# Two attentions in one static schedule: B's loads one transpose at a time, B's query features later to their banks, and new priorities

## The chip, the cores and the metric

The kernel runs on one core of one Trainium2 chip. The metric is the device time of one execution in microseconds (us). The profile is one execution recorded by the hardware profiler. Engine names are those of the profile: PE (matrix engine, PEld its weight loads), DVE (vector), ACT (scalar), POOL (GpSimd) and SP (the queue that issues nearly all DMAs).

## What is computed

Two independent attention layers, A and B, each with 2048 tokens, width 512, 32 heads of 16. Their outputs stand side by side in the result.

```python
# A: full softmax attention
qkv = (x @ wqkv) -> q, k, v per head
p = softmax(q k^T / 4)               # 32 heads x 2048 x 2048
out_A = (p v) @ wo
# B: linear attention with learned features
phi_q = [softmax(q w_phi), softmax(-q w_phi)]     # 32 features per head
phi_k = the same of k
kv, z = sum over s of phi_k v, phi_k
out_B = (phi_q kv / (phi_q z + 1e-6)) @ wo
```

## The kernel before, in words

**A's tiling.** The work of A is cut into 32 units, a unit being 4 heads and 512 queries, `units[u] = (g, c)`. Each unit has 16 key tiles of 128 keys. For one key tile, PE forms the scores of the four heads (L642), the scores are exponentiated, and PE multiplies them with V (L657) into one PSUM bank per unit. Eleven or more of the 16 tiles of a unit go through ACT: `act_kt` makes two halves, each of two score matmuls into one of two bank pairs (`A_bank`, PSUM banks 0 to 3) and one exponential of 128x1024 on ACT (L757). The other tiles go through DVE: `dve_kt` makes four score matmuls into single banks (the pool `G`, banks 4 to 7), four conversions (L795) and three adds (L806) that together approximate the exponential. In the whole program 758 exponentials are on ACT, and 133 tiles (532 conversions, 399 adds) are on DVE.

**The end of a unit.** `make_unit_end` copies the unit's bank to `X` (L704, DVE). Then a chain over the SP queue follows: `sums<-X` (L710, DMA), reciprocal `rin<-sums` (L713, DVE), `scr<-rin` (L716, DMA), four broadcasts `Yd<-scr` (L719, DMA), a multiply on POOL (L726), for odd units four more DMAs `OT<-Oo` (L733), and after 8 units the output projection (L849), its copy (L853) and its store (L857). The reciprocal stands in DVE's own queue, which runs in order, so DVE can do nothing else while that DMA has not landed.

**B's work.** It is laid into A's as filling. `start_b` issues B's loads on SP: the small `BDr` (L901), 8 transposing loads of the query and key weights (L902), 4 transposing loads of B's input, 512 KB each (L905), and two plain loads (L907, L909). They go into buffers that A's projections have just finished with (`w`, `xT`), so they start when A's last projection is done. After them come 8 folds of the feature map into the weights (`fold`, L917 and L921), 16 key steps (`k_step`: L933 features, L936 exponentials, L946 scaling on POOL, L955 values, L966 the sum over keys), and then the query part: `qf_step` (L995 features on PE, L999 exponentials on ACT) and 16 `q_step`s (L1009 on PE, L1019 and L1022 on DVE, L1036 to L1046 on POOL, the transpose L1052 on PE, its copy L1055 on ACT, the output projection L1058 on PE, its copy L1062 on DVE and its store L1065). B's steps are released in proportion to how many of A's 512 key tiles have been placed; the fractions are `B_AT`.

**What sets the order.** `_Sched` places tasks at build time. Each engine has several streams (queues) of tasks with a weight each; for every engine the scheduler takes, among the first tasks of its streams, the one with the smallest start plus weight, with assumed durations and latencies. The order that results is fixed into every engine's instruction queue; on the chip only semaphores are waited for. A task of PE that would delay the next A score pair beyond its due time gets 0.4 added (L238 to L242). Where PE would be idle, matmuls on zeros keep it busy (L684).

**B's load tasks before.** One load task holds all its DMAs, so nothing of A's can stand between them on SP:

```python
return put(sp_b, _Task("sp", us * n, dma(d, lambda e, t, i: fn(e, i), n), deps, lat=lat))   # us=0.5
```

**The query features before.** The PE task of `qf_step` depends on B's input and the folded weights alone and takes a bank of `G`; the two exponentials that free this bank depend in addition on `bs["kend"]`, the end of the key part.

Of the kernel before, what the change touches and what calls it, by code (L numbers as in the profile page):

```python
# [151 lines left out]
class _Sched:  # L152
# [10 lines left out]
    FORCE = 0.40  # L163

    def __init__(self):
        self.free = {}
        self.busy = {}
        self.streams = {}
        self.end = 0.0
        self.mode = None  # L170
        self.rows = [0.0] * 4
        self.port = {"dve": 0.0, "pool": 0.0}
        self.urgent = None
        self.last_port = None
        self.filler = None
        self.active = collections.deque()
        self.nfill = 0
        self.nforce = 0
# [38 lines left out]
    def _choose(self, eng, ss):  # L217
        cand = []
        for s in ss:
            if not s["q"] and s["src"] is not None:  # L220
                s["src"](s)
            if s["q"]:
                t = s["q"][0]
                if t.prep is not None:
                    t.prep(t)
                r = self._ready(t) if t.gate is None or t.gate() else None
                if r is not None:
                    if s is not self.urgent:
                        r += self.SLACK.get(eng, 0.0)
                    st = self._start(t, r)  # L230
                    w = s["w"]
                    cand.append([st, st + (w(t) if callable(w) else w), s, r])
        if not cand:
            return None
        if eng == "pe" and self.urgent is not None:
            u = [c for c in cand if c[2] is self.urgent]
            if u:
                due = max(u[0][3], self.free["act"] - self.MM - self.PE_LAT)  # L238
                for c in cand:
                    t = c[2]["q"][0]  # L240
                    if t.mode != "r" and c[0] + t.dur + self.SWITCH > due + 0.02:
                        c[1] += 0.4  # L242
        c = min(cand, key=lambda c: c[1])
        return c[0], c[2]
# [91 lines left out]

_LOG2E = 1.4426950408889634
# [6 lines left out]
def _main_path(nc, es, P, dsem, flag, A_x, A_wqkv, A_wo, B_x, B_wqkv, B_w_phi, B_wo, out):  # L344
# [6 lines left out]
    B_AT = (0.24, 0.54, 0.95)  # L351
# [80 lines left out]
    pe_qa = SC.stream("pe", -0.02)  # L432
    SC.urgent = pe_qa
    pe_tp = SC.stream("pe", -0.15)
    pe_qd = SC.stream("pe", lambda t: -0.05 if SC.mode == "r" else 0.25)
    pe_pj = SC.stream("pe", -0.03)
    pe_pa = SC.stream("pe", left_in(pt_sl, 2, 0.1))
    pe_pd = SC.stream("pe", left_in(rj_sl, 1, 0.1))
    pe_b = SC.stream("pe", 0.02)
    pe_op = SC.stream("pe", -0.03)  # L440
    one_bank = [pe_tp, pe_pj, pe_b, pe_op, pe_pa, pe_pd]
    ac_ev = SC.stream("act", -0.1)
    ac_xe = SC.stream("act", -0.2)
    ac_ex = SC.stream("act", 0.0)
    dv_x = SC.stream("dve", -0.4)
    dv_xe = SC.stream("dve", -0.3)
    dv_ev = SC.stream("dve", -0.2)
    dv_op = SC.stream("dve", -0.2)
    dv_n = SC.stream("dve", -0.15)
    dv_a = SC.stream("dve", -0.1)  # L450
    dv_ad = SC.stream("dve", 0.0)
# [3 lines left out]
    dv_ek = SC.stream("dve", -0.1)  # L455
# [28 lines left out]
    def put(s, t):  # L484
        s["q"].append(t)
        return t
# [128 lines left out]
    at = []  # L615
    for g in range(1, 4):
        for c in range(4):
            at.append((32 * (g - 1) + 8 + 4 * c, lambda g=g, c=c: proj("k", g, c)))
        at.append((32 * (g - 1) + 10, lambda g=g: proj("q", g, 0)))
    for i in range(12):  # L620
        at.append((22 + 5 * i, lambda i=i: proj("q", i % 4, 1 + i // 4)))
# [12 lines left out]
    state = {"ua": 0, "ud": 0, "n": 0}  # L634
# [112 lines left out]

    def act_kt(u, kt):
        exps = []
        for half in range(2):  # L750
            qk = qk_task(u, kt, half, [("A", A_bank, 1, 1)], lambda t, i: 2 * t.res["A"].idx + i)
            qk_all[u].append(qk)
            put(pe_qa, qk)

            def ex_emit(e, t, qk=qk):
                b = 2 * qk.res["A"].idx
                return e.activation(pT[:, t.res["p"].idx, :], PS[:, b:b + 2, :].rearrange("p a n -> p (a n)"),  # L757
                                    ACT.Exp, scale=0.25)
            exps.append(put(ac_ex, _Task("act", 0.92, one("act", ex_emit), [qk], lat=AL,
                                         need=[("p", pt_sl, 1, 1)], rel=[lambda qk=qk: [qk.res["A"]]])))  # L760
        put(pe_pa, pv_task(u, exps + [v_ready[kt]],
                           lambda h: VP[:, kt, v0(h):v0(h) + 32],
                           lambda r: pT[:, exps[r // 2].res["p"].idx, 512 * (r % 2):512 * (r % 2) + 512],
                           [lambda: [exps[0].res["p"], exps[1].res["p"]]]))
        close(u)
# [59 lines left out]
    def src_d(_):  # L825
        u = max(state["ud"], state["ua"])
        while u < NU and (not d_rem[u] or (u == state["ua"] and len(a_rem[u]) + len(d_rem[u]) < 4)):
            u += 1
        if u >= NU or u > state["ua"] + 1:
            return  # L830
        if u > state["ua"] and len(a_rem[u - 1]) + len(d_rem[u - 1]) > 3:
            return
        state["ud"] = u
        g, c = units[u]
        for n, kt in enumerate(d_rem[u]):
            if k_ready[(g, kt // 4)].done and q_ready[(g // 2, c)].done and vj_ready[(kt, 3)].done:
                dve_kt(u, d_rem[u].pop(n))
                return
# [47 lines left out]
    pe_kf, pe_v, pe_kv, pe_qf, pe_y, pe_t, pe_o = (SC.stream("pe", x) for x in (-0.03,) * 7)  # L886
    dv_f, dv_red, dv_v, dv_kv, dv_y, dv_d, dv_ob = (SC.stream("dve", x) for x in (-0.2, -0.1, -0.12, -0.12, -0.12, -0.12, -0.15))
    dv_mn = SC.stream("dve", 0.05)
    ac_kf, ac_qf, ac_ot = (SC.stream("act", x) for x in (-0.1,) * 3)
# [5 lines left out]
    def b_load(name, fn, n, deps, lat, us=0.5):  # L895
        d = dsem(name)
        return put(sp_b, _Task("sp", us * n, dma(d, lambda e, t, i: fn(e, i), n), deps, lat=lat))

    def start_b():
# [4 lines left out]
            B_wqkv[:, (i // 4) * 512 + (i % 4) * 128:(i // 4) * 512 + (i % 4 + 1) * 128]), 8, freed, 18.0)  # L904
        b_x = b_load("xb", lambda e, i: e.dma_start_transpose(  # L905
            xT[:, i, :], B_x[0][:, i * 128:(i + 1) * 128]), 4, freed, 25.0)
# [5 lines left out]
            mask8[:].unsqueeze(1).unsqueeze(3).broadcast_to([128, 4, 8, 16]), ALU.mult)), [b_bd], pre=[t_m8], lat=GL))  # L912
# [3 lines left out]
        def fold(x, ct):  # L916
            f = put(pe_b, _Task("pe", 0.24, pe_group(4, lambda e, t, i: e.matmul(  # L917
                PS[:, t.res["b"].idx, i * 128:(i + 1) * 128], w[:, i, x * 512 + ct * 128:x * 512 + (ct + 1) * 128],
                BD[:, i, :], start=True, stop=True)), [b_wt, bd], lat=PL, need=[("b", G, 1, 1)]))
# [11 lines left out]
        def k_step(st):  # L931
# [3 lines left out]
                [b_x] + wf[1], [("b", G, 1, 2), ("e", ek_sl, 1, 2)])  # L935
# [9 lines left out]
            for a in range(2):  # L945
# [11 lines left out]
                [b_x, b_wv, bs["vb1"]], [("b", G, 1, 1), ("v", vb_sl, 1, 1)])  # L957
# [35 lines left out]
        def qf_step(cq, t4):  # L993
# [3 lines left out]
                [b_x] + wf[0], [("b", G, 1, 2), ("e", et_sl, 1, 8)])  # L997
            for a in range(2):
                ets[(cq, 2 * t4 + a)] = f, put(ac_qf, _Task("act", 0.49, one("act", lambda e, t, a=a: e.activation(  # L999
                    eT_b[f.res["e"].idx][:, a, :], bank_of(f), ACT.Exp, scale=1.0 - 2.0 * a)),  # L1000
                    [f2] + bs["kend"], lat=AL, rel=[lambda: [f.res["b"]]]))

        def q_step(st):
# [41 lines left out]
            for k in range(2):  # L1045
# [14 lines left out]
                [te, b_wo], [("b", G, 1, 1)])  # L1060
# [1033 lines left out]
```

## Time and profile before

Three runs took 824.21, 830.3 and 833.1 us; the median is 830.3 us. The profiled execution has a span of 829.5 us and a mean granted PE clock of 0.959.

| engine | busy us | share of the span |
|---|---|---|
| PE | 759.9 | 92% |
| ACT | 751.4 | 91% |
| DVE | 736.3 | 89% |
| POOL | 157.3 | 19% |

The profile cuts the span into stretches, and gives for each the busy time of each engine, the granted PE clock (1.00 is full speed) and what the DMA engines moved. Idle time of ACT, which is the length of a stretch less ACT's busy time in it, sums as follows:

| stretch, us | what happens | ACT idle, us |
|---|---|---|
| 0 to 60 | loads, A's first projections | 16.4 |
| 60 to 160 | A, further projections | 2.0 |
| 160 to 195 | A, last projections, B's first loads | 5.8 |
| 195 to 210 | B's input is loaded | 11.1 |
| 210 to 240 | folds, first key step | 6.3 |
| 240 to 790 | A with B's key and query part | 3.6 |
| 790 to 829.5 | last unit of A, last query steps of B | 33.1 |

Mean durations of single instructions (pitch in a row where several follow each other): exponential of A on ACT 0.93 us (13 in 12.05 us), conversion on DVE 0.62 us (4 in 2.47 us), add on DVE 0.63 us (3 in 1.89 us), group of four value matmuls on PE 0.23 us. The issue of a transposing load holds SP for 1.26 us (weights, median of 8) or 2.36 us (input, median of 4).

### The profile page before, as it was taken

What the parts mean: (1) busy time and instruction counts of PE and PEld (TensorE: products, weight loads), DVE (VectorE), ACT (ScalarE), POOL (GpSimd) and SP (SyncE); (2) the same over time, 40 slices, a digit from 0 to 9 for tenths busy, and PEclk for the clock granted to TensorE, in tenths of its full rate; (3) what the DMA queues carried; (4) which work ended last, traced back from release to release, by engine and by line L of the source; (5) the groups of instructions that cost most, each with busy time, mean ns of one, the idle gap of its engine ahead of it and who ended that gap; (6) DMA issues with size and microseconds to landing.
All of it is one profiled execution on the core that took longest, in us unless ns stands there. A gap on an engine that the chain in (4) does not pass through costs nothing.

```text
span 829.5 us, 17394 instructions
## 1 busy us (share of the span) xinstructions
PE 759.9 (92%) x7165; PEld 231.7 (28%) x7249; DVE 736.3 (89%) x1306; ACT 751.4 (91%) x856; POOL 157.3 (19%) x233
## 2 busy tenths in 40 slices
PE   8999999994999998999989999999999999999963
PEld 3332222221222222222222222223332222332231
DVE  2699999884698999989999999999989999999973
ACT  6879999884699999999999999999999999999930
POOL 5211011110112012221121021005222102302051
PEclk9999999997599999999999999999999999999976
DMA  7100000027000000000000000000000010001001
GB/s 150 54 8 9 11 5 8 8 48 168 7 9 10 14 19 15 12 8 11 10 4 9 27 18 9 12 8 18 15 8 18 14 22 17 20 26 31 9 23 51
DMA packets 44154, 19.61 MB, mean 24 GB/s; under 512 B 33312, under 2 KB 42016, under 8 KB 44064
## 3 DMA queue, kind: packets, MB, share of 16 engines
q1 hardware_dynamic: 42480, 17.60, 8.8%
q8 instruction: 59, 0.97, 0.5%
q10 hardware_dynamic: 1584, 0.79, 0.4%
q14 instruction: 31, 0.25, 0.1%
HBM read 7.88 MB, written 4.46 MB: 15 GB/s over the span
## 4 chain that ended last, share of the span: by engine, by line
ACT 59%; PE 24%; DVE 11%; SPq 3%; issue 1%; DMA 1%; POOL 0%; ACTq 0%; POOLq 0%
ACT pT L757 55%; PE PS L642 8%; PE PS L657 7%; DVE rg L795 6%; DVE rg L806 3%; PE PS L570 3%; ACT e_k L936 2%; PE PS L567 1%; ACT eT L999 1%; SPq L905 1%; SPq L902 1%; PE PS L1058 1%; PE PS L684 1%; ACT e_k L1055 1%; PE PS L525 1%
## 5 line engine op out<-in xcount | busy, mean ns | idle before, releaser
L757 ACT ACTIVATE pT<-PS 128x1024 bf16<-128x1024 f32 x758 | 708.6, 1079 | 32.8 <-PE PS L642 28.2
L642 PE MATMUL PS<-QT,KT 32*128 32x512 bf16 x2048 | 352.0, 389 | 21.7 <-ACT pT L757 13.1
L795 DVE TENSOR_SCALAR rg<-PS 128x512 uint16<-128x512 f32 x532 | 340.5, 680 | 18.1 <-PE PS L642 16.1
L806 DVE TENSOR_SCALAR rg<-rg 128x2048 uint16<-128x2048 uint16 x399 | 260.6, 693 | 4.6 <-PE PS L657 4.1
L642 PEld LDWEIGHTS PS<-QT,KT 32*128 32x128 bf16 x2048 | 89.5, 91 | 302.4 <-ACT pT L757 218.0
L657 PE MATMUL PS<-rg,VJ 128*32 128x512 f16 x1596 | 147.9, 389 | 11.0 <-DVE rg L806 10.7
L657 PE MATMUL PS<-pT,VP 128*32 128x512 bf16 x1516 | 151.7, 397 | 2.2 <-ACT pT L757 1.1
L657 PEld LDWEIGHTS PS<-pT,VP 128*32 128x32 bf16 x1516 | 38.3, 94 | 87.4 <-issue 65.8
L726 POOL TENSOR_TENSOR OT<-X,Yd 128x256 bf16<-128x256 f32 x32 | 22.7, 727 | 198.4 <-DVE rg L806 155.3
L946 POOL TENSOR_TENSOR w<-e_k,stat 128x512 bf16<-128x512 bf16 x32 | 33.2, 1056 | 136.1 <-DVE rmin L952 42.6
L657 PEld LDWEIGHTS PS<-rg,VJ 128*32 128x32 bf16 x1596 | 39.0, 95 | 68.4 <-issue 31.5
L657 PE MATMUL PS<-rg,VP 128*32 128x512 f16 x532 | 53.2, 390 | 0.0
L726 POOL TENSOR_TENSOR Oo<-X,Yd 128x256 bf16<-128x256 f32 x32 | 23.1, 738 | 108.1 <-DMA Yd<-scr 55.2
L1036 POOL TENSOR_TENSOR w<-w 128x272 f32<-128x272 f32 x32 | 23.8, 760 | 98.5 <-DVE w L1022 80.3
L570 PE MATMUL PS<-xT,w 128*128 128x512 bf16 x111 | 30.6, 383 | 3.5 <-issue 1.9
L1055 ACT ACTIVATE e_k<-PS 128x512 bf16<-128x512 bf16 x16 | 10.1, 631 | 20.8 <-PE PS L1052 20.8
L684 PE MATMUL PS<-ones_t,zer 128*32 128x512 bf16 x276 | 28.4, 409 | 0.0
L704 DVE COPY X<-PS 128x512 f32<-128x512 f32 x32 | 22.0, 686 | 4.8 <-PE PS L657 3.6
L1022 DVE TENSOR_TENSOR w<-PS,stat 128x408 f32<-128x408 f32 (+1 forms) x48 | 25.2, 526 | 0.6
L1046 POOL TENSOR_TENSOR w<-w,den 128x256 bf16<-128x256 f32 x32 | 19.8, 636 | 31.3 <-DVE rg L806 9.3
L1058 PE MATMUL PS<-woB,e_k 128*128 128x512 bf16 x50 | 17.5, 435 | 4.6 <-issue 1.8
L939 DVE TENSOR_REDUCE stat<-e_k 128x64 f32<-128x1024 bf16 x16 | 19.3, 1209 | 0.1
(85 smaller groups left out, 422.8 us busy)
## 6 DMA issues: line engine op xcount, KB each, us to landing
Yd<-scr SPq DMA_DIRECT2D x128, 32.0 KB, 1.8
out_dram<-OA SPq DMA_DIRECT2D x16, 128.0 KB, 1.7
out_dram<-e_k SPq DMA_DIRECT2D x16, 128.0 KB, 1.7
OT<-Oo SPq DMA_DIRECT2D x64, 16.0 KB, 1.8
w<-in_A_wqkv_dram SPq DMA_DIRECT2D x2, 384.0 KB, 4.9
OT<-in_A_x_dram SPq DMA_DIRECT2D x1, 512.0 KB, 4.6
w<-in_A_wqkv_dram ACTq DMA_DIRECT2D x1, 512.0 KB, 7.7
WOp<-in_A_wo_dram SPq DMA_DIRECT2D x1, 512.0 KB, 6.8
```

The lines of the kernel that those rows point to most:

```text
L570: return e.matmul(bank_of(t), w[:, ct, c0:c0 + 128], xT[:, ct, c * 512:(c + 1) * 512], start=(ct == 0), stop=(ct == 3))
L642: return e.matmul(out_ap, KT[32 * r:32 * r + n, g, kt * 128:(kt + 1) * 128], QT[32 * r:32 * r + n, c, g // 2, :], start=True, stop=True, t ...
L657: return e.matmul(PS[32 * r:32 * r + 32, pvb[u].idx, :], lhs(8 * (g // 2) + 2 * r + g % 2), rhs(r), start=t.res["first"], stop=t.res["last ...
L684: P.op("pe", lambda e, r=r: e.matmul(PS[32 * r:32 * r + 32, pvb[u].idx, :], zer[:], ones_t[:].unsqueeze(1).broadcast_to([128, 4, 128]), st ...
L726: ms.append(put(po_n, _Task("pool", 0.65, one("pool", lambda e, t, cs=cs: e.tensor_tensor(OT[:, c % 2, g // 2, cs] if even else Oo[:, ms[0 ...
L757: return e.activation(pT[:, t.res["p"].idx, :], PS[:, b:b + 2, :].rearrange("p a n -> p (a n)"), ACT.Exp, scale=0.25)
L795: return e.tensor_scalar(rg[:, q0.res["i"].idx, 512 * r:512 * r + 512], PS[:, qk.res["D"].idx, :], ya, yb, ALU.mult, ALU.add)
L806: ad = put(dv_ad, _Task("dve", 0.59, one("dve", lambda e, t, j=j: e.tensor_scalar(rg[:, t.res["j"].idx, :], rg[:, q0.res["i"].idx, :], flo ...
L946: ph.append(put(po_phi, _Task("pool", 1.0, one("pool", lambda e, t, a=a: e.tensor_tensor(pk[ph[0].res["k"].idx][:, 512 * a:512 * a + 512]. ...
L1022: muls.append(put(dv_y, _Task("dve", 0.485, one("dve", lambda e, t, yv=yv, lo=lo, n=n: e.tensor_tensor(ysv[r0.res["y"].idx][:, 136 * lo:13 ...
L1036: ad = [put(po_y, _Task("pool", 0.65, one("pool", lambda e, t, k=k: e.tensor_tensor(y3(0)[:, 2 * k:2 * k + 2], y3(0)[:, 2 * k:2 * k + 2], ...
L1058: o1, o2 = two_step(pe_o, lambda e, t, i: e.matmul(bank_of(t), oT_b[tp.res["t"].idx][:, i, :], woB[:, i, :], start=(i == 0), stop=(i == 3) ...
```

## The change

The change has four parts.

**Loads.** `b_load` makes one task per DMA, with issue times of 1.32 us (weights) and 2.5 us (input) instead of 0.5, so that DMAs of A can stand between them in SP's order:

```diff
-        return put(sp_b, _Task("sp", us * n, dma(d, lambda e, t, i: fn(e, i), n), deps, lat=lat))
+        return [put(sp_b, _Task("sp", us, dma(d, lambda e, t, r, i=i: fn(e, i)), deps, lat=lat)) for i in range(n)]
...
-            B_wqkv[:, (i // 4) * 512 + (i % 4) * 128:(i // 4) * 512 + (i % 4 + 1) * 128]), 8, freed, 18.0)
+            B_wqkv[:, (i // 4) * 512 + (i % 4) * 128:(i // 4) * 512 + (i % 4 + 1) * 128]), 8, freed, 4.0, 1.32)
...
-            xT[:, i, :], B_x[0][:, i * 128:(i + 1) * 128]), 4, freed, 25.0)
+            xT[:, i, :], B_x[0][:, i * 128:(i + 1) * 128]), 4, freed, 8.0, 2.5)
```

**Query features.** The wait for the end of the key part moves from the exponentials to the PE task, so the bank is taken only then:

```diff
-                [b_x] + wf[0], [("b", G, 1, 2), ("e", et_sl, 1, 8)])
+                b_x + wf[0] + bs["kend"], [("b", G, 1, 2), ("e", et_sl, 1, 8)])
...
-                    [f2] + bs["kend"], lat=AL, rel=[lambda: [f.res["b"]]]))
+                    [f2], lat=AL, rel=[lambda: [f.res["b"]]]))
```

**Due time of A's score pairs.** The due time now counts the score pairs that are done but whose exponential is not placed yet, and the surcharge for being late is 0.346:

```diff
-                due = max(u[0][3], self.free["act"] - self.MM - self.PE_LAT)
+                due = max(u[0][3], self.free["act"] + self.EXP * self.ahead() - self.MM - self.PE_LAT - _W["early"])
...
-                        c[1] += 0.4
+                        c[1] += _W["guard"]
```

**Weights and constants.** All stream weights now come from one table `_W` (for instance PE's transposes -0.288 for -0.15, B's folds 0.111 for 0.02, B's output projection 0.067 for -0.03). `B_AT` becomes (0.24, 0.54, 0.917) for (0.24, 0.54, 0.95); A's late query projections are released every 5.753 tiles for 5 (`p2`); `lead` is 2 for 3. A function `third` would let A's score pair take two banks of `G`, if at least `spare` = 9 slots of `G` were free:

```diff
+        if pair + 0.3 < own and sum(x.left == 0 for x in G) >= _W["spare"]:
+            t.need = [("A", G, 2, 1)]
```

## The prediction

> **What bounds the kernel now.** I read the slices first. ACT, DVE and PE all stand at 9 nearly everywhere, so three engines are close to full; a hole at slices 9 to 12 and the end are the exceptions.
>
> ```profile
> PE   8999999994999998999989999999999999999963
> DVE  2699999884698999989999999999989999999973
> ACT  6879999884699999999999999999999999999930
> PEclk9999999997599999999999999999999999999976
> ```
>
> The chain that ended last is 59% ACT, and 55% of the span is one line, A's exponential. From 240 to 790 us ACT idles 3.6 us in all. So this kernel is ACT's 751.4 us of busy time plus ACT's idle time, 78 us, and the change is worth what it takes from or adds to these 78 us.
>
> ```profile
> L757 ACT ACTIVATE pT<-PS 128x1024 bf16<-128x1024 f32 x758 | 708.6, 1079 | 32.8 <-PE PS L642 28.2
> ```
>
> Of the 32.8 us idle before A's exponentials, 28.2 are waits for scores. The timeline shows the largest of them, and what stands behind it (start us, length us, engine, line; in brackets the idle time before it and its releaser):
>
> ```profile
> 190.64 9.43 SPq L905 DMA_TRANSPOSE xT<-in_B_x_dram  x4
> ...
> 190.81 0.68 DVE L704 COPY X<-PS 128x512 f32<-128x512 f32 x1
> ...
> 201.53 0.62 SPq L710 DMA_DIRECT2D sums<-X  x1
> 206.02 0.25 DVE L713 RECIPROCAL rin<-sums 128x16 f32<-128x16 f32 x1 [11.53 <-DMA sums<-X]
> ...
> 206.88 0.62 PE L657 MATMUL PS<-rg,VJ 128*32 128x512 f16 x4 [10.74 <-DVE rg L806]
> ...
> 208.07 2.96 ACT L757 ACTIVATE pT<-PS 128x1024 bf16<-128x1024 f32 x3 [11.08 <-PE PS L642]
> ```
>
> The copy X is done at 191.5, but its DMA waits on SP for four transposes and two plain loads and is issued at 201.5. The reciprocal waits 11.53 us at the head of DVE's queue; PE waits for DVE, ACT for PE. After it the stretches (busy PE, PEld, DVE, ACT, POOL, then the granted clock, DMA share, GB/s) show a second loss:
>
> ```profile
> 195.00:200.00 5.00, 1.14 (x15) 0.20 (x7) 0.00 (x0) 1.99 (x3) 0.00 (x0) 0.91 1.12 218
> 200.00:205.00 5.00, 0.00 (x0) 0.00 (x0) 0.00 (x0) 0.00 (x0) 0.00 (x0) 0.50 0.99 261
> ...
> 215.00:220.00 5.00, 5.00 (x35) 2.40 (x34) 2.81 (x5) 3.43 (x4) 0.00 (x0) 0.50 0.00 0
> 220.00:225.00 5.00, 5.00 (x35) 1.42 (x32) 3.85 (x6) 3.42 (x4) 1.00 (x1) 0.50 0.00 0
> ```
>
> Until about 229 us PE runs at half clock, is full (5.00 of 5.00), and ACT gets only 3.4 of 5. The hole costs ACT 11.1 us at 195 to 210 and 6.3 after it, 17.4 in all.
>
> **What the skill says.** "Perfetto Trace Analysis", section Tensor Engine Instruction, calls ACT, DVE and GpSimd strict first-in first-out; the 11.53 us at the reciprocal agree. "DMA: Bandwidth & Descriptors", Queues, rings and completion order, says each DMA engine consumes descriptors in ring order; this agrees with `sums<-X` landing 4.47 us after its issue at 201.5 (chain of waits), against at most 2.4 for the last unit (issued 793.25, used 795.69). The same page, Latency and other measured facts, gives 261 GB/s for a transposing DMA; the row at 200 to 205 moves 261. "TensorE: Matmul & The Clock Gate", What's actually happening, states half clock after an idle window of about 3.4 us and full clock after a busy one. The fall agrees (0.50 from 200 us on), the recovery doesn't: it took some 22 us of busy PE. I price with the trace.
>
> **The change part by part.** Work is not changed: both orders hold 758 exponentials, 532 conversions, 399 adds, the same DMAs; only the zero matmuls differ (292 for 276). Steady ACT work therefore stays at 751.4 us, and each part is priced in ACT idle.
>
> *Loads, with the new time of release.* In the new order of SP, unit 5's `sums<-X` stands behind three weight transposes, unit 6's behind the third input transpose, with the fourth after it. The wait this adds is SP's: what queues behind a transpose is the next A DMA, and DVE's reciprocal waits for that. Unit 5 in the worst case: 3 x 1.34 us issue (10.71 / 8), 0.6 own issue, 4.5 landing = 9.1, against 4.4 us of DVE work that the new order has between the copy and the reciprocal (7 instructions of about 0.62), so 4.7 stall. Unit 6: 2.4 + 0.6 + 4.5 = 7.5 against 4.6, so 2.9. Best case for both is 0, for the scheduler now knows 1.32 and 2.5 us per issue. I take 1.5 each, 3 in all (0 to 8). B's consumers have room: the first fold stands about 6.9 us of DVE work (6 conversions, 5 adds) and more after unit 5's reciprocal, while the last two weight transposes need 0.35 + 2.6 + 2.7 = 5.7 us from there; the first key step comes 24 exponentials (22 us) after the first fold. Without a long PE hole the half clock and its 6.3 us go too. Gain 17.4 - 3 = 14.4.
>
> *Start and projections (weights, `p2`).* ACT idles 24.2 us up to 195 us, at least 8 of it before anything can be exponentiated (first A exponential at 11.5 us). PE is 96% busy up to 160 us, so PE's order sets it. In the new order 84 projection matmuls instead of 100 stand ahead of the 32nd exponential's scores (16 x 0.216 = 3.5 us of PE), and up to the 160th there are 24 value matmuls (6 groups x 0.23 = 1.4), 9 DVE scores (about 0.1 each, 0.9) and 56 zero matmuls (14 groups x 0.23 = 3.2) fewer: 5.5 us. The long bursts of projections that cause the gaps at 120.7, 161.2 and 176.2 us (1.8, 2.35, 2.29 us) are broken up. Between 3 and 12; I take 8.
>
> *Query features.* The key part's last sums stood behind exponential 498, the first feature at 508: already after the key part. In the new order they stand at 406 and 429. The moved wait finds its semaphores reached in both; it costs nothing and frees nothing. The key part itself is denser (195 to 406 for 191 to 498).
>
> *Due time, surcharge, `third`.* `third` can never fire: it asks for 9 free slots and `G` has 4. The looser due time lets more work between A's score pairs: pairs of neighbouring gaps with over 1.6 us of other PE work (counted in the two orders, at the pitch the trace gives each matmul) number 67 against 58 (over 2.0: 38 against 21), 36 against 14 of them at exponentials 200 to 450. Before, 3.6 us ACT idle came with these; I add 3 (0 to 6).
>
> *The end.* ACT idles 33.1 us after 790. The query transposes are 5 us apart there (their copies on ACT at 796.0, 800.9, 805.9, 811.5, 816.6). After A's last scores the old order has 5 transposes left, the new one 6, the first of them with its inputs made earlier; A's own chain (copy X at 792.5, output projection at 811.2) is as long. The earlier `B_AT` end doesn't shorten it: in the new order seven query steps start at 438 to 607, nine from 720 on. Cost 0 to 5; I take 2.
>
> Sum: 14.4 + 8 - 3 - 2 = 17.4 us. From the median of 830.3: 812.9.
>
> **The rivals.** *The stall moves (0.17).* Both reciprocals wait 4 us and the half clock returns for 6.3: 14.3 of the 17.4 remain, gain 3.1; start 8, minus 3 and 2: 6.1, so 824.2. For it: SP still serves A and B in order, and the real arrival may drift from the schedule. Against: 4.4 and 4.6 us of DVE work now stand in between, 3.2 before the long wait. *Everything comes (0.15).* 17.4 + 12, nothing lost: 29.4, so 800.9. For it: the start gaps are single waits behind bursts. Against: the denser key part. *Slower than before (0.08).* Nine query steps crowd the end; each takes 5 us, 45 in all against 38 exponentials x 0.93 = 35, and ACT's in-order copies hold A's exponentials up for 10; the end grows by 5; stall remains as above (+3.1), start +3, middle -2: 10.9 slower, 841.2. For it: two of those copies stand only 3 exponentials apart. Against: DVE and POOL have room there (POOL 12.6 of 20 us busy at 790 to 810).
>
> **How the numbers follow.** The forecast has 0.60. The range from 802 to 826 takes in the second case and nearly the first in its bounds; the slower case lies outside. Faster than 822 by the forecast, the fast case and part of the moved stall: 0.80; within 1%: 0.12; slower: 0.08.
>
> **What would show it.** In the changed profile: no zero in the slices at 195 to 210, PE clock 1.00 there, reciprocal waits for `sums<-X` under 5 us in sum (step one); ACT idle up to 195 us near 16 (start); ACT idle between 240 and 790 near 7; after A's last exponential the end near 40 us. I am wrong if DVE still waits over 8 us for a DMA near B's loads, or if ACT loses over 10 us among the crowded query steps near the end.

## The result, and the profile after

The changed kernel takes 800.2 us (median of 4 runs, 793.95 to 802.11), the kernel before beside it 829.6 (824.21 to 833.1). The ratio is 0.964 with a 95% interval from 0.956 to 0.971. The forecast was 812.9 with a range from 802 to 826, so the time fell just below the range: the direction was right, the size was not. 29 us came where 17.4 were forecast. The ratios and their intervals, here and below, leave out single executions that ran over 1.5% longer than the shortest of the same kernel.

The slices of the changed kernel, in the order PE, ACT, granted PE clock, DMA:

```profile
PE   8999999999999999999899999999999999999963
ACT  6899999999999999999898999999999999999930
PEclk9999999999999999999888999999999999999987
DMA  6100000045000000000000000000000000000011
```

The 4 that PE and ACT showed at slice 10 before is gone (the slices are too wide to show a zero there), and DMA still shows B's loads at slices 9 and 10. What is left is one thin place at slices 20 to 22, with a lower clock, and the end. The chain that ended last and the group of A's exponentials:

```profile
ACT 85%; PE 11%; DVE 2%; issue 1%; POOL 1%; POOLq 0%; ACTq 0%
...
L797 ACT ACTIVATE pT<-PS 128x1024 bf16<-128x1024 f32 x758 | 706.2, 1079 | 6.9 <-PE PS L652 4.9
```

ACT's share of the chain rises from 59% to 85%: hardly anything but ACT itself is left to wait for. The exponentials are as many (758) and as long (1079 ns); the idle time before them falls from 32.8 to 6.9 us. The timeline of SP and DVE about B's loads shows why (start us, length us, engine, line; SP's lengths lump several issues together):

```profile
162.08 3.76 SPq L943 DMA_TRANSPOSE w<-in_B_wqkv_dram  x3
165.89 0.61 SPq L720 DMA_DIRECT2D sums<-X  x1
166.54 4.24 SPq L943 DMA_TRANSPOSE w<-in_B_wqkv_dram  x3
...
183.73 1.84 SPq L946 DMA_TRANSPOSE xT<-in_B_x_dram  x1
185.61 0.60 SPq L720 DMA_DIRECT2D sums<-X  x1
186.65 1.83 SPq L946 DMA_TRANSPOSE xT<-in_B_x_dram  x1
```

```profile
168.94 0.24 DVE L723 RECIPROCAL rin<-sums 128x16 f32<-128x16 f32 x1
...
187.96 0.25 DVE L723 RECIPROCAL rin<-sums 128x16 f32<-128x16 f32 x1 [0.25 <-DMA sums<-X]
```

A's two DMAs now stand between B's transposes. Unit 5's reciprocal doesn't wait at all and unit 6's waits 0.25 us, where one of them waited 11.53 before. Stretch by stretch (busy us of PE, PEld, DVE, ACT, POOL, then granted clock, DMA share, GB/s; ACT's idle time is the length less the fourth number):

```profile
0.00:60.00 60.00, 56.79 (x398) 17.93 (x404) 38.90 (x63) 49.12 (x60) 20.26 (x44) 1.00 0.29 73
60.00:160.00 100.00, 97.68 (x878) 26.63 (x890) 98.13 (x170) 100.00 (x110) 14.49 (x20) 1.00 0.04 9
160.00:195.00 35.00, 33.78 (x354) 10.35 (x346) 33.90 (x59) 35.00 (x39) 4.17 (x5) 1.00 0.58 129
195.00:240.00 45.00, 43.18 (x432) 12.56 (x434) 44.98 (x77) 44.98 (x53) 9.05 (x10) 1.00 0.06 17
240.00:480.00 240.00, 225.10 (x2369) 66.72 (x2394) 222.06 (x390) 234.26 (x274) 51.44 (x61) 0.96 0.05 13
480.00:700.00 220.00, 211.54 (x2120) 59.67 (x2128) 217.27 (x384) 219.99 (x246) 26.27 (x40) 1.00 0.06 15
```

From 60 to 195 us ACT doesn't idle at all, nor from 195 to 240. The two profiled spans (829.5 and 798.4) can be laid side by side in ACT's time:

| part | before, us | after, us | gain | forecast |
|---|---|---|---|---|
| ACT idle, 0 to 195 (start) | 24.1 | 10.9 | 13.2 | 8 |
| ACT idle, 195 to 240 (hole, half clock) | 17.4 | 0.0 | 17.4 | 14.4 |
| ACT idle, 240 to 700 | 3.5 | 5.7 | -2.2 | -3 (middle) |
| ACT idle, 700 to the end | 33.1 | 32.4 | 0.7 | -2 (end) |
| ACT busy | 751.4 | 749.4 | 2.0 | 0 |
| span | 829.5 | 798.4 | 31.1 | 17.4 |

(The forecast cut its middle at 790 us instead of 700; before, the two cuts differ by 0.1.) After A's last exponential, at 760.9 us, 37.5 us follow, against 38.0 before.

### The profile page after: what moved, and what is told of

Its sections match the earlier page's. It is cut to its first block, busy times and chain, and to the rows that moved or that the text cites. A ratio compares the mean times of both kernels' runs of the same rounds, so it can differ in the third digit from the quotient of the medians.

```text
span 798.4 us, 17434 instructions
## 1 busy us (share of the span) xinstructions
PE 746.1 (93%) x7197; PEld 221.1 (28%) x7265; DVE 732.9 (92%) x1306; ACT 749.4 (94%) x856; POOL 158.5 (20%) x233
## 4 chain that ended last, share of the span: by engine, by line
ACT 85%; PE 11%; DVE 2%; issue 1%; POOL 1%; POOLq 0%; ACTq 0%
ACT pT L797 81%; PE PS L652 2%; PE PS L667 2%; ACT e_k L977 2%; ACT eT L1040 1%; PE PS L1099 1%; PE PS L890 1%; PE PS L576 1%; PE PS L534 1%; ACT e_k L1096 1%; PE PS L1050 0%; PE PS L579 0%; DVE rg L847 0%; ACT Wf L1040 0%; DVE e_k L1103 0%
## 5 line engine op out<-in xcount | busy, mean ns | idle before, releaser
L797 ACT ACTIVATE pT<-PS 128x1024 bf16<-128x1024 f32 x758 | 706.2, 1079 | 6.9 <-PE PS L652 4.9
L652 PE MATMUL PS<-QT,KT 32*128 32x512 bf16 x2048 | 344.1, 386 | 19.3 <-ACT pT L797 12.4
L836 DVE TENSOR_SCALAR rg<-PS 128x512 uint16<-128x512 f32 x532 | 336.8, 678 | 14.9 <-PE PS L652 13.9
L652 PEld LDWEIGHTS PS<-QT,KT 32*128 32x128 bf16 x2048 | 85.5, 91 | 306.3 <-ACT pT L797 236.2
L667 PE MATMUL PS<-pT,VP 128*32 128x512 bf16 x1516 | 147.7, 391 | 1.3 <-ACT pT L797 0.8
L736 POOL TENSOR_TENSOR OT<-X,Yd 128x256 bf16<-128x256 f32 x32 | 23.6, 758 | 143.8 <-DVE rg L847 115.2
L579 PE MATMUL PS<-xT,w 128*128 128x512 bf16 x114 | 34.7, 383 | 3.1 <-issue 2.1
L1096 ACT ACTIVATE e_k<-PS 128x512 bf16<-128x512 bf16 x16 | 10.2, 639 | 20.1 <-PE PS L1093 19.9
L890 PE MATMUL PS<-WOp,OT 128*128 128x512 bf16 x55 | 18.9, 440 | 1.6 <-issue 1.6
```

The source lines that it names most:

```text
L579: return e.matmul(bank_of(t), w[:, ct, c0:c0 + 128], xT[:, ct, c * 512:(c + 1) * 512], start=(ct == 0), stop=(ct == 3))
L652: return e.matmul(out_ap, KT[32 * r:32 * r + n, g, kt * 128:(kt + 1) * 128], QT[32 * r:32 * r + n, c, g // 2, :], start=True, stop=True, t ...
L667: return e.matmul(PS[32 * r:32 * r + 32, pvb[u].idx, :], lhs(8 * (g // 2) + 2 * r + g % 2), rhs(r), start=t.res["first"], stop=t.res["last ...
L736: ms.append(put(po_n, _Task("pool", 0.65, one("pool", lambda e, t, cs=cs: e.tensor_tensor(OT[:, c % 2, g // 2, cs] if even else Oo[:, ms[0 ...
L836: return e.tensor_scalar(rg[:, q0.res["i"].idx, 512 * r:512 * r + 512], PS[:, qk.res["D"].idx, :], ya, yb, ALU.mult, ALU.add)
L890: first, t = two_step(pe_op, lambda e, t, p, st=st: e.matmul(bank_of(t), OT[:, c % 2, p, st * 128:(st + 1) * 128], WOp[:, p, :], start=(p ...
```

## The experiments

All times are medians over all executions, beside runs of the kernel before on the same chip, which itself took 825.4 to 829.3 us there; so small differences are read from the ratios. None of these kernels leaves out a part of the computation. The "package" is the whole change, the "due rule" its third part (due time and surcharge), and "the minimum" is explained with the second group of runs. The table gives for each profiled execution ACT's idle time in three stretches, when A's last exponential ends, how long the kernel still runs then ("tail"), and how many of the 32 exponentials of B's query features are still to come at that moment.

| run | time, us | ratio (95%) | 0-195 | 195-240 | 240-700 | A's end | tail | to come |
|---|---|---|---|---|---|---|---|---|
| before | 829.6 | | 24.1 | 17.4 | 3.5 | 791.5 | 38.0 | 4 |
| after | 800.2 | 0.964 (0.956-0.971) | 10.9 | 0.0 | 5.7 | 760.9 | 37.5 | 4 |
| sums_moved | 818.5 | 0.987 (0.981-0.992) | 23.7 | 0.9 | 9.0 | 778.8 | 38.0 | 4 |
| durations_only | 822.4 | 0.992 (0.989-0.995) | 24.1 | 2.5 | 4.6 | 777.3 | 37.9 | 4 |
| loads_only | 830.6 | 1.002 (0.999-1.005) | 23.6 | 0.0 | 6.2 | 761.2 | 64.5 | 12 |
| loads_mn | 819.1 | 0.989 (0.986-0.992) | 27.8 | 1.1 | 6.1 | 790.0 | 33.9 | 0 |
| before_mn | 831.9 | 1.003 (1.000-1.007) | 23.7 | 11.1 | 12.5 | 807.5 | 31.1 | 0 |
| features_only | 868.1 | one run | 23.5 | 16.7 | 7.3 | 766.7 | 99.7 | 32 |
| features_mn | 831.7 | 1.002 (0.999-1.005) | 23.7 | 17.0 | 2.9 | 799.0 | 30.9 | 0 |
| loads_due_mn | 813.2 | 0.980 (0.971-0.988) | 18.2 | 1.9 | 10.1 | 784.3 | 29.9 | 0 |
| after_oldw_mn | 806.9 | 0.977 (0.970-0.984) | 15.8 | 0.2 | 3.1 | 772.2 | 30.2 | 0 |
| after_old_due | 824.2 | 0.993 (0.989-0.995) | 20.9 | 0.6 | 1.2 | 755.8 | 58.0 | 12 |
| after_mn | 803.9 | 0.971 (0.966-0.976) | 11.8 | 0.0 | 2.3 | 769.2 | 31.5 | 0 |
| after_mn_p2 | 808.2 | 0.978 (0.972-0.984) | 12.0 | 0.0 | 7.7 | 776.6 | 30.2 | 0 |
| all_but_loads | 848.7 | 1.018 (1.010-1.027) | 23.5 | 5.6 | 13.3 | 771.0 | 77.8 | 20 |
| searched | 794.1 | 0.962 (0.956-0.967) | 10.9 | 2.5 | 1.4 | 756.8 | 36.0 | 4 |

### Is the hole the order on SP? (sums_moved, durations_only)

The kernel before with one DMA moved in SP's finished order, to the place after the first of B's input transposes:

```diff
+    sp = P.streams["sp"].items
+    i0 = [i for i, x in enumerate(sp) if x[2] == "d_xb" or x[2] == "xb"]
+    i1 = [i for i, x in enumerate(sp) if x[2] == d_s1[0] and i > i0[-1]][0]
+    it = sp.pop(i1)
+    sp.insert(i0[0] + 1, it)
```

> The kernel before, with one DMA moved: unit 6's sums<-X stands after the first of the four input transposes instead of after all four and two plain loads. All other orders are unchanged. Theory S (the hole is made by the place in SP's queue, and the half clock follows from the hole): the DMA is issued near 193 us, lands some 4.5 us later, the reciprocal waits 2 to 4 us instead of 11.5, PE never idles for 5 us, the clock stays at 1.00 at 205 to 229, and of the 17.4 us ACT idle at 195 to 240 some 12 to 15 go: about 816. Rival R1 (the DMA engines are full with transposes, so any small DMA behind the first one waits for all): the wait stays at 9 to 11 us, about 828. Rival R2 (the half clock has another cause than the hole, the folds): only the hole goes, the clock is still 0.50 there: about 822.

And the kernel before with its load tasks whole, but with their true durations told to the scheduler:

```diff
-            B_wqkv[:, (i // 4) * 512 + (i % 4) * 128:(i // 4) * 512 + (i % 4 + 1) * 128]), 8, freed, 18.0)
+            B_wqkv[:, (i // 4) * 512 + (i % 4) * 128:(i // 4) * 512 + (i % 4 + 1) * 128]), 8, freed, 4.0, 1.32)
...
-            xT[:, i, :], B_x[0][:, i * 128:(i + 1) * 128]), 4, freed, 25.0)
+            xT[:, i, :], B_x[0][:, i * 128:(i + 1) * 128]), 4, freed, 8.0, 2.5)
```

> The kernel before with one task per load as before (nothing of A's can stand between the transposes), but with the issue times and latencies of the changed kernel (1.32 and 2.5 us per DMA, 4 and 8 us). Theory K (what was missing is that the scheduler did not know the durations): the order now has 9.0 us of DVE work between unit 6's copy and its reciprocal, so the reciprocal waits under 2 us, the hole and the half clock go: about 813. Rival I (interleaving is needed): A's DMAs wait all the same, and work behind the reciprocal runs dry: ACT still loses 8 us or more at 180 to 240, about 822 or more.

With one DMA moved, DVE's wait for `sums<-X` and the stretches that were empty read:

```profile
DVE rin L713 <- DMA sums<-X: 1.2, 1, 1.2
```

```profile
195.00:210.00 15.00, 13.31 (x145) 4.79 (x148) 14.68 (x26) 14.15 (x16) 0.01 (x1) 1.00 0.78 178
210.00:240.00 30.00, 29.00 (x306) 8.51 (x298) 27.44 (x47) 30.00 (x36) 7.90 (x9) 1.00 0.04 9
```

The same transposes run at the same time (178 GB/s), and the hole and the half clock behind it are gone: 17.4 us of idle become 0.9. The moved DMA stands between transposes, and the reciprocal starts 2.4 us after its issue (192.47 to 194.87), so it is not the busy DMA engines that held it before. The time falls by 1.3% (some 11 us), less than the 16.5 us, since this execution loses 5.5 us more at 240 to 700. With the durations alone, SP still issues all four input transposes in one row (190.71 to 200.66), and `sums<-X` after them at 201.11, as late as before. But the scheduler, which now knows this, has put 9.0 us of other DVE work before the reciprocal, and the wait is 1.6 us. ACT's idle time at 195 to 240 us falls to 2.5; the median gains 0.8%, some 7 us, and the profiled execution was the shortest of the seven. So the hole is the reciprocal at the head of DVE's queue, and two cures remove it; letting A's DMAs in between the transposes is one of them, not a condition.

### The loads alone (loads_only, loads_mn, before_mn)

The first is the load part of the change alone, as its diff in the section on the change shows it, in the kernel before.

> The kernel before with the load part of the change alone: one task for each transposing DMA, with a duration of 1.32 or 2.5 us and a lead of 4 or 8 us; features, due rule and weights as before. The prediction gave this part a gain of 17.4 - 3 = 14.4 us. Theory S (the hole is the queue of SyncE and nothing else): ACT idle from 160 to 240 us falls from 23.2 to 4 to 9 us, the reciprocals wait under 3 us for their sums, and the time lies where moving one DMA and correcting the durations alone put it, 814 to 824 us, since other stages of the new order may take back some of it. Rival (the loads need the new weights around them): idle from 160 to 240 stays above 14 us and the time is 825 us or more.

The hole is gone completely (0.0 of 17.4 us, a wait of 0.3 us), and nothing is gained. A's last exponential ends at 761.2 us, 30 us earlier than before, and then ACT's timeline shows B's query part, which should long be done:

```profile
764.46 1.09 ACT L999 ACTIVATE Wf<-PS 128x512 bf16<-128x512 f32 x2 [3.27 <-PE PS L995]
...
786.03 1.08 ACT L999 ACTIVATE eT<-PS 128x512 bf16<-128x512 f32 x2 [13.02 <-PE PS L995]
```

Both theories on record missed this. In the instruction order, B's query steps stop after the sixth (near exponential 650 of 750), and the other ten come after A's end. The suspect is the running minimum `rmin`, an instruction of some 0.2 us in each key and query step that keeps the smallest reciprocal so far: it is on a DVE stream of its own with the worst weight of all (`dv_mn`, +0.05), and gives back the statistics slots without which no further query step starts. The scheduler takes it only if DVE has nothing better to do. The trace fits: the fourth query step's minimum comes at exponential 625, the fifth's after the last, the 750th, and with two slots four finished steps allow six. The second run has the loads and this weight alone, the third the weight alone:

```diff
-    dv_mn = SC.stream("dve", 0.05)
+    dv_mn = SC.stream("dve", -0.2)
```

> The kernel before with the load part of the change alone, and the running minimum's DVE stream at -0.2 instead of +0.05. Theory M (what ate the loads' gain in the run of the loads alone was that the running minimum, which gives back the statistics slots of B's query steps, is not chosen before A's end): all query steps lie before A's last exponential, which ends 30 to 32 us before the end; the hole is gone (160 to 240 us loses 4 to 8 us), and the time is 809 to 818 us, the 14 to 17 us of the prediction's load term below before_mn. Rival E (the loads alone crowd B's query part out for another reason, and need the rest of the package): the last exponential ends 45 us or more before the end and the time is above 820 us.

> The kernel before with the running minimum's DVE stream at -0.2 instead of +0.05 and nothing else, as the control. 762 exponentials on ACT for 758, so some 4 us more of ACT, and all query steps before A's end, so a tail of 30 to 32 us for 38. Theory M: the hole at 195 to 210 us stays (160 to 240 us loses 18 to 24 us), the time is 824 to 833 us, no more than 5 us from the kernel before. Rival: if the weight alone made the difference, 815 us or less.

With the weight changed, no query feature is left after A's end and the time falls from 830.6 to 819.1. The weight by itself brings nothing (831.9; the reciprocal still waits 10.8 us for `sums<-X` behind B's loads). So the starved minimum had eaten the gain, and where it is out of the way the loads are worth the difference of the two ratios, 1.003 - 0.989, or some 12 us: under the forecast's 14.4 and the 14 to 17 expected. (In the profiled execution of loads_mn the clock is 0.96 already in the first 195 us, and that of before_mn has a mean clock of 0.953; their idle times beyond the hole are not used. features_mn, with its 17.0 us and the same weight, shows the hole undisturbed.)

### The query features alone (features_only, features_mn)

The moved wait alone in the kernel before, and then with `dv_mn` at -0.2:

```diff
-                [b_x] + wf[0], [("b", G, 1, 2), ("e", et_sl, 1, 8)])
+                [b_x] + wf[0] + bs["kend"], [("b", G, 1, 2), ("e", et_sl, 1, 8)])
...
-                    [f2] + bs["kend"], lat=AL, rel=[lambda: [f.res["b"]]]))
+                    [f2], lat=AL, rel=[lambda: [f.res["b"]]]))
```

> The kernel before with the second part alone: the feature matmuls wait for the end of the key part, the exponentials don't. The prediction priced this at nothing: 830. The order of the instructions says otherwise: all 16 query steps stand behind A's last exponential (the 748th), since the update of the running minimum (L952), which the end of the key part waits for, is never chosen before A runs out. Theory M (the minimum's low priority holds the query part back once the features hold no banks): hole as before, 10 exponentials and 21 us of query work less before A's end, then 16 query steps at 4 to 5 us: about 855 to 875.

> As features_only, with one weight changed: the running minimum's stream at -0.2 for 0.05. Theory M: the query part is no longer held back, its last transpose stands at exponential 727 of 764, and only A's own chain is left at the end: ACT idle after A's last exponential falls from 33 us to 24 to 28; the hole stays; 6 more exponentials on ACT: about 826. Rival (the bank wait itself slows B or A): over 835.

The forecast called this part free. Alone it costs some 40 us (868.1 in one run, against 828.3 beside it): all 32 query exponentials come after A's end, as ACT's timeline shows.

```profile
754.63 12.09 ACT L757 ACTIVATE pT<-PS 128x1024 bf16<-128x1024 f32 x13
768.19 4.03 ACT L999 ACTIVATE eT<-PS 128x512 bf16<-128x512 f32 x8 [1.46 <-PE PS L995]
...
791.74 4.51 ACT L999 ACTIVATE eT<-PS 128x512 bf16<-128x512 f32 x8 [9.04 <-PE PS L995]
```

It is the same inversion of priorities: the features now wait for the end of the key part, which includes the minimum. With the minimum served early the cost is gone (831.7), and so is every use of the part: the hole stays at 17.0 us. In the package, putting the wait back onto the exponentials gives the very same program, instruction for instruction, so there it neither costs nor brings anything. Why the kernel before escapes the inversion was not tried. What its order suggests, and no more, is that features that hold banks of `G` leave DVE's conversions without banks at times, and so leave DVE free for the minimum.

### The start: due rule, weights, constants (loads_due_mn, after_oldw_mn, after_mn, after_mn_p2)

loads_due_mn is the kernel before with loads, features and the due rule (0.346 as in the change), old weights and constants, and `dv_mn` -0.2.

> The kernel before with three parts of the change (loads, query features, due time and surcharge of A's score pairs), all old weights and constants, except the running minimum's weight at -0.2. Theory D (loads and due time bring nearly all; the table of weights matters in that it does not starve B's query part): ACT idle up to 195 us near 11 to 14, no hole, all query steps done before A ends (last transpose at exponential 715 of 762): 800 to 806. Rival W (the weights bring the start's gain): ACT idle up to 195 us stays at 20 to 24, 810 or more.

after_oldw_mn is the changed kernel with all old stream weights (the constants stay new), after_mn the changed kernel as it is, and after_mn_p2 that with one constant back; all have the minimum at -0.2. after_oldw_mn:

```diff
-_W = dict(tp=-0.288, qa=-0.02, qd_r=-0.032, qd_o=0.261, pj=-0.051, pa_n=2, pa_w=0.053, pd_n=0, pd_w=0.055,
-          b=0.111, op=-0.039, dx=-0.396, dxe=-0.31, dev=-0.248, dop=-0.201, dn=-0.245, da=-0.1, dad=0.006,
-          dek=-0.101, av=-0.057, kf=-0.03, v=-0.03, kv=-0.03, qf=-0.03, y=-0.046, t=-0.03, o=0.067, df=-0.2,
+_W = dict(tp=-0.15, qa=-0.02, qd_r=-0.05, qd_o=0.25, pj=-0.03, pa_n=2, pa_w=0.1, pd_n=1, pd_w=0.1,
+          b=0.02, op=-0.03, dx=-0.4, dxe=-0.3, dev=-0.2, dop=-0.2, dn=-0.15, da=-0.1, dad=0.0,
+          dek=-0.1, av=-0.1, kf=-0.03, v=-0.03, kv=-0.03, qf=-0.03, y=-0.03, t=-0.03, o=-0.03, df=-0.2,
...
```

after_mn and after_mn_p2:

```diff
-          dred=-0.1, dv=-0.11, dkv=-0.098, dy=-0.011, dd=-0.112, dob=-0.124, dmn=0.059, akf=-0.155, aqf=-0.1,
+          dred=-0.1, dv=-0.11, dkv=-0.098, dy=-0.011, dd=-0.112, dob=-0.124, dmn=-0.2, akf=-0.155, aqf=-0.1,
```

and, in after_mn_p2 alone:

```diff
-          p2=5.753, lone=0)
+          p2=5, lone=0)
```

> The kernel after, but with every stream weight at the value that the kernel before has (PE, DVE, ACT), the running minimum's DVE stream at -0.2 (so that it is not starved), and the rest of the change kept: loads, features, due rule, and the new constants (the projections of query columns spaced 5.753 pairs apart for 5, and the hand-over constants). The start lost 24.1 us of ACT before (0 to 195 us), 10.9 after, 18.2 with the due rule alone and 20.9 with the weights alone. Theory C: the spacing of the projections and the due rule are what the start needs; then idle from 60 to 195 us is 0 to 2 us, the first 195 us lose 11 to 13, and the time is 803 to 810. Rival W: the weights are needed too (they order the projections against the scores); then idle from 60 to 195 is 4 to 7 us and the time 810 to 816.

> The changed kernel with one weight changed: the running minimum's stream at -0.2 for 0.059. Its query steps no longer pause between exponentials 620 and 720; the last transpose stands at 701 of 766 instead of behind the end. Theory T (the end is A's own chain of DMAs, not B's query steps): ACT idle after A's last exponential only falls from 32 to 25 to 28 us, while 8 more exponentials (7.4 us) and 6 more copies and 4 feature exponentials (5 us) stand on ACT before the end: 796 to 804, no clear difference. Rival B (B's query steps set the end): idle after the end falls below 20: 790 or less.

> The kernel after with the running minimum's weight at -0.2 (which measured 803.9 us with 0.4 us of ACT idle from 60 to 195 us) and one constant back at its old value: the query projections spaced 5 pairs apart instead of 5.753. Theory C (the spacing matters at the start): 60 to 195 us loses 3 to 7 us, time 807 to 812. Rival W (the weights and the due rule do it, the spacing does nothing): 60 to 195 us loses 0 to 1.5 us, time 802 to 806.

What ACT loses up to 195 us falls from 23.7 (neither: features_mn) to 18.2 with the due rule (between the 11 to 14 and the 20 to 24 that the two theories expected), to 15.8 with the due rule and the new constants, and to 11.8 with the weights too. The new weights and constants without the due rule leave 20.9 (after_old_due, below). So the spacing `p2` was the wrong suspect: at its old value the start loses 12.0 for 11.8, and the first theory of after_oldw_mn and after_mn_p2 falls by its idle times, though both times (806.9 and 808.2) lie in the ranges that it gave. (after_mn_p2 is slower by 0.7% all the same, with 5.4 us more idle at 240 to 700; its interval overlaps that of after_mn.) Counted from the kernel before, the due rule gives 5.9 us of the start, weights and constants together 3.2, and all of them 13.2, more than the sum (loads, features and the minimum's weight alone leave 23.5 to 23.7, so they bring 0.6 at most).

### The due rule, and the loads taken out of the package (after_old_due, all_but_loads)

```diff
-                due = max(u[0][3], self.free["act"] + self.EXP * self.ahead() - self.MM - self.PE_LAT - _W["early"])
+                due = max(u[0][3], self.free["act"] + 0.0 - self.MM - self.PE_LAT - _W["early"])
...
-          aot=-0.285, spare=9, early=0.0, guard=0.346, cut=4, lead=2, b0=0.24, b1=0.54, b2=0.917, p0=8, p1=22,
+          aot=-0.285, spare=9, early=0.0, guard=0.4, cut=4, lead=2, b0=0.24, b1=0.54, b2=0.917, p0=8, p1=22,
```

> The changed kernel with the old due time and surcharge (no count of finished score pairs, 0.4). Theory D: the projections come in bursts again: up to the 160th exponential 56 matmul groups of PE work as before (132 us against 128), ACT idle at 60 to 195 us rises from 0 to 4 to 8, while 0 to 60 stays near 11; six query steps are crowded behind A's end (nine transposes after the last score): end longer by 10 to 15: 815 to 825. Rival W (the weights alone make the start): ACT idle at 60 to 195 under 2.

all_but_loads is the changed kernel with the load lines of before.

> The changed kernel with the loads as before (one task for each load, 0.5 us per DMA). Theory S: a reciprocal waits over 8 us for its DMA behind the transposes, PE falls to half clock, ACT loses 12 to 20 us at 160 to 240. Besides, the order differs: B's query part starves after its second step and 14 query steps stand behind A's 752nd and last exponential, which adds some 35 us: 840 to 860. Rival: no hole, ACT idle at 160 to 240 under 5 (the other parts had already moved the units away from the loads).

Each of these takes away nearly the whole gain or more, and not only in the stage in which its own part acts. Without the due rule the profiled span grows by 15.4 us: 10.0 at the start, 0.5 behind it, 14.1 after 700 us with 12 query exponentials to come, less 4.6 in the middle and 4.7 of ACT's busy time (752 exponentials); the medians differ by 24, and this execution was the shortest of twenty. Its trace shows how the rule acts at the start: from 60 to 195 us ACT waits 0.9 to 3.2 us at six places, and just before five of them PE has 5 to 9 projection matmuls; with the rule no wait there reaches 0.7 us. Without the loads the span grows by 50.5: 12.6 up to 195 us, 5.6 behind it, 7.6 in the middle, 27.2 after 700 us with 20 query exponentials to come, less 2.5 of busy time. The reciprocal waits 5.7 us there, not the 8 and more that were expected, and earlier, in the stretch from 160 us, with the clock at 0.77:

```profile
160.00:195.00 35.00, 22.32 (x201) 5.28 (x197) 20.34 (x35) 22.18 (x24) 3.15 (x4) 0.77 0.56 125
```

### The end (after_mn), and a version that is no slower (searched)

In the changed kernel nine of sixteen query steps crowd the end. after_mn tests whether they set it. There no query exponential is left after A's end, the tail shrinks from 37.5 to 31.5 us, and nothing is gained: A's last exponential comes 8.3 us later (769.2). ACT is busy for 10.7 us more before it, with 8 more of A's exponentials (766 for 758) and with the 4 query exponentials and 6 copies that used to follow, and idles 2.4 us less. What remains, 31.5 us, more than the 25 to 28 expected, is A's own chain. So the end is an exchange between B's query steps behind A's end and A's tiles before it, not a loss of its own.

searched is the changed kernel with five numbers moved a little (`qd_r` -0.038, `pd_w` 0.095, `dx` -0.286, `aqf` -0.06, `p2` 5.53).

> The kernel after with five weights moved a little (quadrant matmuls in r mode -0.038 for -0.032, left-over quadrant weight 0.095 for 0.055, DVE x stream -0.286 for -0.396, query-feature ACT stream -0.06 for -0.1, query projection spacing 5.53 for 5.753). The order planned for it ends 2.0 us earlier than that of after. Theory P (what the planner sees is what the chip does): 797 to 800 us, 0 to 2 us below after's 800.2. Rival N (such small moves of weights are below what the granted clock does from order to order): 799 to 806 us, no better than after.

It took 794.1 us (793.5 to 795.0), below both ranges on record, but its ratio, 0.962 (0.956 to 0.967), can't be told from the change's 0.964: the kernel before took only 825.4 beside it. It is as good as the change, and not shown to be better.

## Why the prediction was right or wrong

**The loads: mechanism right, residue too large.** That the queue of SP behind four transposes held DVE, then PE and ACT, and that the half clock goes with the hole, is shown by sums_moved: one DMA moved, 16.5 of 17.4 us of idle gone. The residue of "1.5 each, 3 in all" measured 0.25 us in sum. The landing of 4.5 us was put down to the transposes, and they don't cause it: behind one transpose it took 2.35 us with the issue (185.61 to 187.96), and behind all four, in durations_only, 2.05 (201.11 to 203.16). In the kernel before two plain loads of 512 KB stood right before the DMA, and they landed at 204.75 and 206.18, about when the reciprocal started (206.02); behind the same two loads it took 4.40 us in before_mn and 4.75 in features_mn. What the transposes cost is the queue of SP, which they hold while they are issued (9.43 us for the four). As a part alone the loads brought some 12 us, but only once the minimum was out of the way.

**The start: the step that failed.** "Between 3 and 12; I take 8" measured 13.2, outside its own bounds (ACT idle up to 195 us is 10.9, not near 16). The step asked what the weights and `p2` do to PE's order. Weights and constants without the due rule give 3.2 us, the low bound, and `p2` beside the rest 0.2. The due rule was priced in the middle alone, as a loss of 3, and so put at nothing for the start; it gives 5.9 us there with the old weights, and 4.1 more together with the new ones. A rule that lets projections go before a score pair that ACT doesn't need yet acts where projections are many, and that is the start: without it ACT waits there behind bursts of projections (after_old_due). Of the forecast's shortfall of 13.7 us (31.1 for 17.4) this is 5.2.

**The rest of the shortfall:** 3.0 from the residue, 2.7 at the end, 2.0 of ACT busy time that the forecast held constant, 0.8 in the middle.

**The middle: right in size.** 2.2 us lost for 3 forecast. But 5.6 of the 5.7 us of idle in the changed kernel lie in two places with a half clock (see below), and the new orders without the due rule's term lose 1.2 there, so whether it is the rule's looser spacing or the clock that costs this is argued, not shown.

**The end: wrong sign, and the wrong question.** "Cost 0 to 5; I take 2" measured a gain of 0.7. The forecast's test, an end near 40 us after A's last exponential, held (37.5). But the risk at the end was neither one transpose more nor the crowding. Four of the runs (features_only, loads_only, after_old_due, all_but_loads) left 12 to 32 of B's query exponentials behind A's end, which cost up to 36 us (features_only against features_mn). The rival "slower than before" had the place right and the cause wrong.

**The query features: right in the package, for an incomplete reason.** "It costs nothing and frees nothing" holds there. As a statement about the edit it is wrong by some 40 us (features_only), since the moved wait includes the running minimum's, and this minimum has the lowest priority on DVE. That the wait costs nothing was read from a finished order in which the wait is long reached, and not from the scheduler, for which it is one more dependence on a stream that is served last.

**The sum.** Adding the parts was itself a weak step. The parts alone come to +2 (loads), +40 (features) and, with the minimum mended, to -10 for the loads alone and -16 for loads, features and due rule; taken out of the package they are worth some 24 (due rule) and 45 us (loads), by the ratios. The orders of the two finished programs, from which the forecast took most of its numbers, were the better guide. The rival "everything comes", 800.9, took the start at its upper bound and no losses, and lies within 1 us of the measurement; the start was larger still and the middle did lose, so its sum is right by luck, and its terms are not.

## What to carry to other kernels

Where a scheduler builds the order, price an edit on the finished orders and not part by part, and ask of every rule that changes priorities in which stage its work is most plentiful. Before a wait is moved onto a task, look at the weakest stream that it waits for: an instruction of 0.2 us with the lowest priority held back the whole query part. And a DMA issue that stands in one queue with large transposes should either be let in between them or have its consumer placed later: one removed 16.5 of the 17.4 us of idle time, the other 14.9.

## What the runs showed of the hardware

**A half clock without an idle gap.** In the changed kernel PE's clock falls at 387 us and again at 415. The stretches about the first (same columns as above):

```profile
382.00:384.00 2.00, 1.51 (x24) 0.46 (x24) 1.72 (x4) 2.00 (x4) 1.80 (x2) 1.00 0.00 0
384.00:386.00 2.00, 1.54 (x38) 0.52 (x34) 2.00 (x4) 2.00 (x4) 0.27 (x1) 1.00 0.00 0
386.00:388.00 2.00, 1.62 (x22) 0.50 (x22) 2.00 (x5) 2.00 (x3) 0.00 (x0) 0.89 0.03 8
388.00:390.00 2.00, 1.67 (x11) 0.30 (x10) 2.00 (x5) 1.56 (x2) 0.00 (x0) 0.50 0.00 0
390.00:392.00 2.00, 2.00 (x7) 0.33 (x6) 0.24 (x2) 1.52 (x3) 0.00 (x0) 0.50 0.00 0
392.00:394.00 2.00, 2.00 (x22) 0.75 (x24) 0.69 (x1) 1.13 (x3) 0.00 (x0) 0.50 0.00 0
394.00:396.00 2.00, 2.00 (x27) 0.47 (x19) 1.28 (x3) 1.35 (x2) 0.00 (x0) 0.90 0.00 0
```

The longest gap of PE just before is 0.37 us. PE was 75% to 81% busy in each row up to 388 us, in part with the 128x34 matmuls of B's sums over keys, and that came before the half clock. The Trainium skill ("TensorE: Matmul & The Clock Gate", What's actually happening) ties the throttle to how busy PE has been recently; its "idle window" of about 3.4 us is not a window without work here. Which measure decides is not shown: PE was busy 2.57 of the 3.4 us before this fall and 2.85 of the 3.4 before the next, while the kernel before kept its full clock with 2.65 of 3.5 (326.5 to 330). Only after the fall does ACT, until now full, lose time (0.44 to 0.87 of each 2 us). The half clock lasted 6.8 us here, 10.2 us from 415 on, and 30.7 us in the kernel before (199.1 to 229.8), where PE was full for the last 22.9.

**The spread of one program goes with the clock.** Executions of the same kernel with 20 runs each (loads_only, loads_mn, before_mn, features_mn, after_old_due) follow a line in their mean granted clock, with correlations from -0.96 to -0.99 and a slope of -5.8 to -6.4 us for each 0.01 of clock. 0.01 of 820 us is 16.4 us at half clock, so a microsecond at half clock goes with about 0.37 us of time, by this estimate. That the clock is the cause, and not something that lowers both, is not tested. The changed kernel's fastest run (793.95 us) had 0.990, its slowest (802.11) 0.975; from before to after the profiled clock rises from 0.959 to 0.978, or from 68 to 35 us at half clock. As an estimate with the same slope, these 33 us are 12 of the 31 gained; they would be a part of the idle time in the table above, not an addition to it.
